# x tiles on multiples of 512 bytes, and another order of small work around them: a gated linear-attention layer on one Trainium2 core

## The chip, the cores and the metric

The kernel runs on one core of one Trainium2 chip. The metric is the device time of one execution in microseconds. The engines are TensorE (PE; its weight loads are listed apart as PEld), VectorE (DVE), ScalarE (ACT), GpSimd (POOL) and SyncE (SP), which issues most of the DMAs. L1160 means line 1160 of the kernel before.

## The reference

The input x has 2,048 tokens of 640 features. It is normalised per token, and two branches read the result:

```python
xn = _layernorm(x, axis=-1)
s = _A_ref(xn, A_wqkv, A_w_phi, A_wo)
g = _silu(_B_ref(xn, B_w1, B_b1, B_w2, B_b2))
return x + s * g
# _A_ref: 32 heads of 20
pq = jnp.einsum("bhsd,hdf->bhsf", q, w_phi)      # the same for k
phi_q = jnp.concatenate([_softmax(pq, axis=-1), _softmax(-pq, axis=-1)], axis=-1)
kv = jnp.einsum("bhsf,bhsd->bhfd", phi_k, v)
z  = jnp.einsum("bhsf->bhf", phi_k)
o = phi_q kv / (phi_q z + 1e-6)                  # then @ wo
# _B_ref: 640 -> 1536 -> 640
h = _gelu(jnp.einsum("bsd,df->bsf", x, w1) + b1)
return jnp.einsum("bsf,fd->bsd", h, w2) + b2
```

All inputs and outputs are fp32.

## The kernel before, in words

Every fp32 operand of a large product is split into a high and a low part, and each product is done in three passes (high by high, high by low, low by high: `PASSES`). Many products are done by a block scheme that needs sums of blocks of x and of the weights and fewer matmuls: a `Unit` with the steps s1 to s7 in the first stage and the query stage, seven `PARTS` in the feed-forward units.

The transposed, normalised x and its block sums lie in two tiles that stay on the chip for most of the run: `xp` (8 blocks, high and low, 512 columns each) and `xd` (9 blocks, in the place of the folded weights `folds`). A small unused tile, `xpad`, stands ahead of them in their pool. A partition of the on-chip memory is filled in this order: constants, 23 slabs of 5,120 bytes, 11 rows of 2,816 bytes, the small tiles, then `xpad`, `xp`, `xd`. By the tiles' sizes xp begins at byte 158,656 of a partition, which is 309 x 512 + 448. Late in the run the x pool is closed, and an equal pad, `lpad`, and the pool `late` (13 tiles of up to 5,120 bytes) take the place: the output weights `wo` and every second set of `oT` lie there.

The stages, in time:

- The first stage (to about 180 us) folds w_phi into the weights, normalises and transposes x, and makes keys, values and the state `kv`. `turn` transposes and splits a pair of tokens' tiles, `t_sums`, `t_hi` and `t_lo` make the block sums in xd, `weight_sums` (`vw`, `kw`) and `weight_forms` (`kform`, `vform`) those of the weights. `norm_a`, `norm_b` and `norm_apply` are the statistics and the application of the layer norm.
- The query stage (to about 249 us) makes the query features: a maximum (`q_max`, `p_max`), a negation (`f_neg`), a subtraction (`q_sub`, `p_sub`), an exponential and a store (`q_put`). Four tiles are done plainly (`query_plain`), the others in units.
- The gated stage (to about 577 us) runs 12 feed-forward units. Each has 54 matmuls in `part` (L1160: x streams past the weights `w1s`) and 60 in `down` (L1189: `hs` streams past `w2s`).
- The output stage runs four chunks of 512 tokens. `finish` (L1361) streams `oT` past `wo`; `oT` of the first and third chunk lies in `late`, that of the second and fourth in slabs.

The order of work is written out by hand: under the manual schedule every engine and queue does its work in the order of the program. A unit calls `slot(i)` between its steps, and tables (`k_side`, `v_side`, `q_side`, `first_q`, `second_q`, `mid_q`) say which small work goes into which slot. SyncE's loads and stores are a queue of that kind too. In a unit, cx1 (L499), cu2 (L502) and c22 (L505, L506) read the bank of a step before a later step writes it.

Of the kernel before, what the change touches and what calls it, by code (L numbers as in the profile page):

```python
# [45 lines left out]
def hedgehog_gated_mlp_kernel(ctx: ExitStack, tc: tile.TileContext, x, xt_in, wqk, bd, wv, wo, w1, b1, w2, b2, out_t):  # L46
# [6 lines left out]

    xstack = ExitStack()
    xpool = xstack.enter_context(tc.tile_pool(name="xpool", bufs=1))
    xpool.tile([P, 16], F32, name="xpad")
    xp = xpool.tile([P, 8, 2, CW], F32R, name="xp")
    foldt = xpool.tile([P, 2 * KC * 6 * P + 6 * 120], F32, tag="D", name="folds")
    folds = foldt[:, :2 * KC * 6 * P].rearrange("p (w c i t) -> p w c i t", w=2, c=KC, i=6)
# [24 lines left out]
    def bankA():  # L84
        return pools["A"].tile([P, 2, 512], F32, tag="A", name="pA")
# [177 lines left out]
    def t_hi(q):  # L263
        nc.scalar.activation(xd()[:, :, 0, at(q)], tts[q][:], AF.Copy)

    def t_lo(q):
        tt, dst = tts.pop(q), xd()[:, :, :, at(q)]
        nc.gpsimd.tensor_tensor(dst[:, :, 1, :], tt[:], dst[:, :, 0, :].bitcast(F32), op=OP.subtract)

    def turn(q, part, ps=None):  # L270
        if part == 0:
            xrs[q] = slab(F32, "xr", (P, KC, W2))[:]
        xr = xrs[q]
        if ps is None:
            ps = bankW()[:]
        srcs = [(0, k) for k in range(4)] if part == 0 else [(1, k) for k in range(4)] if part == 1 else [(0, 4), (1, 4)]
        for i, (o, k) in enumerate(srcs):
            nc.tensor.transpose(ps[:, i * P:(i + 1) * P], xns[2 * q + o][:, k * P:(k + 1) * P], ident[:])
        v = ps.rearrange("p (k t) -> p k t", t=P)
        if part == 0:  # L280
            raw, src, dst = xr[:, 0:4, :P], v, xp[:, 0:4, :, at(q)]
        elif part == 1:
            raw, src, dst = xr[:, 0:4, P:], v, xp[:, 5:7, :, at(q)]
        else:
            raw, src, dst = xr[:, 4, :].rearrange("p (k t) -> p k t", t=P), v[:, :2], xp[:, 4::3, :, at(q)]
            xns.pop(2 * q), xns.pop(2 * q + 1)
        hi = src[:, 2:4] if part == 1 else src
        nc.scalar.activation(dst[:, :, 0, :], hi, AF.Copy)
        nc.scalar.activation(raw, src, AF.Copy)
        nc.vector.tensor_tensor(dst[:, :, 1, :], hi, dst[:, :, 0, :].bitcast(F32), op=OP.subtract)  # L290
# [97 lines left out]
    def key_fin(ef, at=None):  # L388
        ss = head_sums(ef, "rc")
        rc = ss[:] if at is None else at  # L390
        nc.vector.reciprocal(rc, ss[:])
        scale_heads(ef, rc, nc.gpsimd if at is None else nc.vector)
        return ef
# [339 lines left out]
    vw = weight_sums(rv01, rv23)  # L733
    fold_q(3)
    phis[2] = key_fin(es.pop(2), tiny[:, 64:128])
    turn(2, 2, bankA()[:, 0])
    x_in(8)
    x_in(9)
    t_sums(2)
    next(vw)  # L740
    norm_a(7)
    kv_acc(1, phis.pop(1), vs.pop(1))
    fold_q(4)
    es[3] = feat1(pk, tiny[:, 32:64])
    t_hi(2)
    t_lo(2)
    next(vw)
    vs[3] = value(3)
    next(kform)
    feat2(es[3])  # L750
    norm_b(7)
    next(vw)
# [52 lines left out]
    def k_acc(p):  # L805
        for o in range(2):
            kv_acc(2 * p + o, flat(uk[p].out[o]), uv[p].out[o])
        del uk[p], uv[p]
# [15 lines left out]
    def k_side(p):  # L824
        o = p - 1
        if p == 2:
            return {
                0: [(x_in, 10), (k_form,)],
                1: [(turn, 3, 0), (turn, 3, 1), (v_form,), (v_rows, 2)],
                3: [(turn, 3, 2), (k_form,), (x_in, 11)],  # L830
                5: [(t_sums, 3), (norm_a, 8), (v_form,)],
            }
        if p == 3:
            return {
                0: [(k_neg, 2, 0), (k_max, 2, 0, True), (x_in, 13), (turn, 4, 2), (k_neg, 2, 1), (t_sums, 4)],
                1: [(v_rows, 3)],
                2: [(k_sub, 2, 0, nc.vector), (k_max, 2, 1, False), (x_in, 12), (t_hi, 4), (norm_apply, 11), (t_lo, 4), (k_sub, 2, 1, nc.gpsimd)],
                4: [(norm_apply, 10), (k_exp, 2, 0)],
                5: [(k_sum, 2, 0)],
                6: [(k_scale, 2, 0)],  # L840
            }
        return {
            0: [(k_acc, p - 2), (k_neg, o, 0), (k_neg, o, 1), (k_max, o, 0, True), (p < 7 and t_sums, p + 1), (p == 7 and load_rq,)],
            1: [(p == 4 and x_in, 14), (p == 4 and x_in, 15)],
            2: [(k_sub, o, 0, nc.vector), (v_rows, p), (k_max, o, 1, False), (p < 7 and t_hi, p + 1), (k_sub, o, 1, nc.gpsimd)],
            4: [(p < 7 and t_lo, p + 1), (k_exp, o, 0)],
            5: [(k_sum, o, 0), (k_scale, o, 0)],
        }

    def v_side(p):  # L850
        o = p - 1
        if p == 2:
            return {
                0: [(norm_b, 8)],
                1: [(acc3,), (norm_a, 9), (t_hi, 3), (norm_apply, 8)],
                3: [(norm_b, 9), (t_lo, 3)],
                4: [(spill, 2), (norm_apply, 9), (norm_a, 10), (v_form,)],
                5: [(norm_a, 11), (turn, 4, 0)],
                6: [(norm_b, 10), (turn, 4, 1), (v_form,), (norm_b, 11)],
            }  # L860
        if p == 3:
            return {
                0: [(turn, 5, 0), (norm_a, 12)],
                1: [(k_exp, 2, 1)],
                2: [(k_sum, 2, 1), (k_scale, 2, 1), (turn, 5, 1)],
                3: [(norm_b, 12), (norm_a, 13)],
                4: [(norm_b, 13), (turn, 5, 2)],
                5: [(norm_apply, 12), (norm_apply, 13), (spill, 3)],
            }
        return {  # L870
            0: [(p < 6 and turn, p + 2, 0), (p == 4 and norm_a, 14), (k_exp, o, 1)],
            2: [(k_sum, o, 1), (p < 6 and turn, p + 2, 1)],
            3: [(k_scale, o, 1), (p == 4 and norm_b, 14), (p == 4 and norm_a, 15)],
            5: [(p == 4 and norm_apply, 14), (p < 6 and turn, p + 2, 2), (p == 4 and norm_b, 15)],
            6: [(p == 4 and norm_apply, 15)],
        }
# [37 lines left out]
    def q_side(q):  # L914
        e0, e1 = uq[q].out
        return {
            0: [(f_neg, e0), (f_neg, e1), (q_max, e0, (q, 0)), (q_sub, e0, (q, 0), nc.gpsimd)],
            2: [(q_max2, q)],
            3: [(q_sub, e1, (q, 1), nc.vector)],
            4: [(q_put, e0, 2 * q)],  # L920
            5: [(q_put, e1, 2 * q + 1)],
        }

# [34 lines left out]
    def wq_form(n):  # L958
        t = slab(F32R, "wsum")
        t4 = t[:].rearrange("p b (k c) -> p b k c", k=2)  # L960
        for k in range(2):
            src = {"S1": rq[k][:, HALF:], "S2": sums["st"][:, 1, k * HALF:(k + 1) * HALF],
                   "S3": sums["st"][:, 0, k * HALF:(k + 1) * HALF], "S4": rq[2 + k][:, :HALF]}[n]
            split_sum(src, [t4[:, b, k] for b in range(2)], nc.gpsimd)
        sums[n] = [lambda b, t4=t4, i=i: t4[:, b, i] for i in range(2)]
# [12 lines left out]
    def p_max(t, psum=False):  # L978
        f_neg(pl[t])
        q_max(pl[t], t, pls[t][:, HALF:HALF + 64] if psum else None)  # L980
# [36 lines left out]
    k_exp(o, 1)  # L1017
    k_sum(o, 1)
    wq_form("S2")
    pl[2] = query_plain(2)  # L1020
    q_put(pl[0], 0)
    k_scale(o, 1)
    p_max(1, True)
    p_sub(1, nc.vector)
    pl[3] = query_plain(3)
    q_put(pl[1], 1)
    wq_form("S1")
    p_max(2, True)
    p_sub(2, nc.vector)
    wq_form("S4")  # L1030
    k_acc(o)
    w1r = load_w1(0)
    fq = {}
# [12 lines left out]

    def first_q():
        return {
            0: [(p_max, 3, True)],
            1: [(q_put, pl[2], 2), (p_sub, 3, nc.vector)],  # L1050
            5: [(q_put, pl[3], 3)],
            6: [(w1_step,)],
        }

    def second_q():
        return {
            2: [(w1_step,)],
            5: [(kv_end,)],
        }

    def mid_q(i):
        q = order[i - 2]
        e0, e1 = uq[q].out
        return {
            0: [(f_neg, e0), (f_neg, e1), (q_max, e0, (q, 0)), (q_sub, e0, (q, 0), nc.gpsimd)],
            2: [(q_max2, q), (w1_step,)],
            3: [(q_sub, e1, (q, 1), nc.vector)],
            4: [(q_put, e0, 2 * q)],
            5: [(q_put, e1, 2 * q + 1), (i == 2 and load_xq, 3)],
        }  # L1070

    fq.update(wq_forms())
# [17 lines left out]
    slot(2)  # L1090
    u.s3()
    u.cu2()
    slot(3)
    slot(4)
    w.s6()
    w.c21()
    u.s4()
    slot(5)
    u.s5()
    u.c22()  # L1100
    f_neg(ea[0])
    q_max(ea[0], 0)
    q_sub(ea[0], 0, nc.gpsimd)
# [301 lines left out]
    for unit in range(units):  # L1405
# [79 lines left out]
        if not more:  # L1485
            phin = load_phi(ORDER[1])
            xstack.close()
            ctx.enter_context(tc.tile_pool(name="pad", bufs=1)).tile([P, 16], F32, name="lpad")
            late = ctx.enter_context(tc.tile_pool(name="late", bufs=13, reuse_waits="tile"))
        w1f = w1_forms(w1r) if more and not back else none  # L1490
        if back:
# [125 lines left out]
```

## Time and profile before

| | |
|---|---|
| time, median of 3 runs | 682.1 us (680.92 to 682.28) |
| the profiled execution's own time | 681.68 us |
| its span, first to last instruction | 679.9 us |
| granted TensorE clock over the span | 0.997 |
| PE, DVE, ACT, POOL busy | 98%, 67%, 47%, 58% |
| DMA | 129.60 MB, 191 GB/s over the span |

The span is what the trace shows; the time of the execution has 1.8 us more around it. A timeline or chain row gives a start and a length in us, the engine, the line, the tile written and the tiles read, and the number of instructions that were merged; a bracket behind it gives the idle time of the engine ahead of it and what ended that. A row of the chain of waits gives the total, the number and the longest in us.

### The profile page before, as it was taken

To read this page: it belongs to the slowest core of one execution; us is meant where nothing else is said; L and a number is where in the kernel's file an instruction comes from. 1 tells how busy PE (TensorE), PEld (TensorE's weight loads), DVE (VectorE), ACT (ScalarE), POOL (GpSimd) and SP (SyncE) were. 2 spreads that over 40 slices of the span, in tenths; PEclk is the share of its full clock that TensorE was granted. 3 is DMA by queue.
4 is the path that set the end of the run, shared out by engine and by line. 5 is a ranking of instruction groups with operands and counts; after the bars stand their busy time and mean duration, and the time that the engine had idled before them with its cause. 6 is when DMAs were issued, how large, how long until landed. Compare 5 with 4: busy or idle time off the path is not lost.

```text
span 679.9 us, 11969 instructions
## 1 busy us (share of the span) xinstructions
PE 667.8 (98%) x4615; PEld 576.5 (85%) x4615; DVE 453.3 (67%) x716; ACT 322.8 (47%) x552; POOL 391.9 (58%) x341
## 2 busy tenths in 40 slices
PE   9999899999999999999999999999999999999997
PEld 9999799999999987888888888888888886777875
DVE  4968897766775657485875775767867876333232
ACT  3556676654566667534244147632132346645220
POOL 2777787765774442956875844636357665322232
PEclk9999899999999999999999999999999999999999
DMA  8436560032732881719657595296375185657444
GB/s 332 174 117 195 171 182 10 2 98 80 210 117 98 286 325 49 266 60 320 220 174 278 209 425 240 65 366 227 133 278 196 76 323 200 227 182 274 151 149 139
DMA packets 76408, 129.60 MB, mean 191 GB/s; under 512 B 4768, under 2 KB 44192, under 8 KB 75456
## 3 DMA queue, kind: packets, MB, share of 16 engines
q1 hardware_dynamic: 76032, 128.19, 53.4%
q10 hardware_dynamic: 320, 0.66, 0.5%
q8 instruction: 36, 0.59, 0.4%
q14 instruction: 20, 0.16, 0.1%
HBM read 81.97 MB, written 46.20 MB: 189 GB/s over the span
## 4 chain that ended last, share of the span: by engine, by line
PE 90%; POOL 3%; ACT 2%; DVE 2%; issue 2%; DMA 1%; DVEq 0%; ACTq 0%; POOLq 0%
PE pB L1189 24%; PE pB L1160 22%; PE pW L453 18%; PE pB L1361 10%; PE pA L312 3%; PE pB L1292 3%; PE pW L936 2%; PE pB L1281 2%; PE pA L157 2%; PE kv L547 1%; DMA xq<-xp_dram 1%; PE pA L623 1%; POOL rk L655 1%; POOL tt L249 1%; POOL wv L132 1%
## 5 line engine op out<-in xcount | busy, mean ns | idle before, releaser
L1189 PE MATMUL pB<-hs,w2s 128*128 128x512 f32 x720 | 167.8, 391 | 0.0
L1189 PEld LDWEIGHTS pB<-hs,w2s 128*128 128x128 f32 x720 | 134.5, 188 | 30.2 <-issue 1.2
L1160 PE MATMUL pB<-xp,w1s 128*128 128x512 f32 x324 | 83.3, 394 | 0.0
L1160 PE MATMUL pB<-xd,w1s 128*128 128x512 f32 x324 | 81.4, 394 | 0.0
L1160 PEld LDWEIGHTS pB<-xd,w1s 128*128 128x128 f32 x324 | 60.6, 187 | 15.0
L1160 PEld LDWEIGHTS pB<-xp,w1s 128*128 128x128 f32 x324 | 60.6, 187 | 14.7
L1198 DVE TENSOR_TENSOR y<-pB,y 128x512 f32<-128x512 f32 x100 | 63.8, 680 | 12.8 <-PE pB L1189 12.7
L1361 PE MATMUL pB<-oT,wo 128*128 128x512 f32 x300 | 72.1, 395 | 0.0
L370 POOL TENSOR_TENSOR eq<-eq,rc 128x1280 f32<-128x1280 f32 x16 | 37.9, 2370 | 58.8 <-DVE rc L1260 51.2
L1165 ACT ACTIVATE pB<-pB,b1t 128x512 f32<-128x512 f32 x48 | 31.8, 662 | 78.7 <-DVE pB L1461 26.9
L1361 PEld LDWEIGHTS pB<-oT,wo 128*128 128x128 f32 x300 | 55.4, 188 | 15.0 <-DVE oT L1296 1.2
L351 POOL TENSOR_TENSOR e<-e,mxs 128x1280 f32<-128x1280 f32 x13 | 30.7, 2369 | 56.3 <-ACT e L357 18.5
L453 PE MATMUL pW<-wsum,xd 128*128 128x320 f32 x288 | 49.4, 310 | 1.2 <-DVE wsum L419 1.0
L571 POOL TENSOR_TENSOR w1s<-raw,w1s 128x640 fp32r<-128x640 f32 (+1 forms) x18 | 24.4, 1356 | 42.2 <-ACT w1s L570 42.2
L1247 POOL TENSOR_TENSOR ez<-eq,zrep 128x1280 f32<-128x1280 f32 x16 | 47.3, 2955 | 0.0
L357 ACT ACTIVATE e<-e 128x1280 f32<-128x1280 f32 x32 | 40.7, 1271 | 13.0 <-DVE e L351 4.6
L453 PEld LDWEIGHTS pW<-wsum,xd 128*128 128x128 f32 x288 | 43.6, 188 | 1.8 <-DVE wsum L419 1.2
L1176 ACT ACTIVATE x<-pB 128x512 f32<-128x512 f32 x12 | 7.2, 598 | 75.4 <-PE pB L1160 75.4
L1284 ACT ACTIVATE ph<-pB 120x512 f32<-120x512 f32 (+1 forms) x48 | 23.6, 561 | 34.8 <-PE pB L1281 31.7
L370 POOL TENSOR_TENSOR e<-e,rc 128x1280 f32<-128x1280 f32 x15 | 36.1, 2406 | 6.3 <-DVE rc L799 3.0
L1171 DVE TENSOR_TENSOR hs<-pB,hs 128x512 fp32r<-128x512 f32 x48 | 32.0, 685 | 5.4 <-ACT hs L1167 5.4
L1367 POOL TENSOR_TENSOR xres<-y,xres 128x256 f32<-128x256 f32 x20 | 14.2, 732 | 35.8 <-DVE y L1366 17.4
(204 smaller groups left out, 1322.0 us busy)
## 6 DMA issues: line engine op xcount, KB each, us to landing
raw<-in_w_dram SPq DMA_DIRECT2D x42, 320.0 KB, 5.5
e_dram<-e SPq DMA_DIRECT2D x16, 640.0 KB, 3.5
eq<-e_dram SPq DMA_DIRECT2D x16, 640.0 KB, 7.5
phi_dram<-eq SPq DMA_DIRECT2D x16, 640.0 KB, 3.3
phi<-phi_dram SPq DMA_DIRECT2D x16, 640.0 KB, 8.0
xt<-in_x_dram SPq DMA_DIRECT2D x16, 320.0 KB, 5.8
xres<-in_xt_dram SPq DMA_DIRECT2D x20, 256.0 KB, 5.4
out_dram<-xres SPq DMA_DIRECT2D x18, 256.0 KB, 4.8
```

The costliest lines, as they stand in the source:

```text
L351: eng.tensor_tensor(e3, e3, mx[:, :, None].to_broadcast([P, 64, DH]), op=OP.subtract)
L357: nc.scalar.activation(ef, ef, AF.Exp)
L370: eng.tensor_tensor(e3, e3, rc[:, :, None].to_broadcast([P, 64, DH]), op=OP.mult)
L453: nc.tensor.matmul(self.bank[ch][:, :HALF], self.x(blk, a), w(b), start=new and i == 0, stop=i == len(mms) - 1, skip_group_check=True)
L571: nc.gpsimd.tensor_tensor(sl[:, 1, :n], src, sl[:, 0, :n].bitcast(F32), op=OP.subtract)
L1160: nc.tensor.matmul(bank[ch][:], tl[:, a, off + wo_:off + wo_ + P], mov(blk, b), start=new and n == 0, stop=n == len(mms) - 1, skip_group_c ...
L1165: nc.scalar.activation(ps, ps, AF.Gelu_apprx_tanh, bias=b1t[:, f:f + 1])
L1171: nc.vector.tensor_tensor(hs[:, 1], ps, hs[:, 0].bitcast(F32), op=OP.subtract)
L1189: nc.tensor.matmul(ps[:], ws[i][:, b, d * P:(d + 1) * P], hs[o][i][:, a, :], start=i == n == 0, stop=(i, n) == (GF - 1, 2), skip_group_che ...
L1198: nc.vector.tensor_tensor(y, ps[:], y, op=OP.add)
L1247: nc.gpsimd.tensor_tensor(zv, ef, zf, op=OP.mult)
L1361: nc.tensor.matmul(ps[:], w, o, start=n == 0, stop=n == 14)
```

## The change

The pads ahead of the x tiles and of `late` grow from 16 to 32 floats, so that xp, xd and the tiles of `late` begin at multiples of 512 bytes of a partition. The rest puts existing work in another order:

- first stage: two steps of the value weights' sums (`next(vw)`) and one of the key weights' forms (`next(kform)`) earlier; `norm_apply(11)` ahead of `t_hi(4)`; `acc3` one slot earlier; `turn(4, 0)` ahead of `norm_a(11)`;
- query stage: `p_max(1)` ahead of `query_plain(2)`, the form S1 behind S4, `p_sub(3)` and `kv_end` one slot earlier, one negation of a unit in slot 1, `load_xq(3)` ahead of a `q_put`, and in the last unit `u.s5` ahead of `u.s4` and c22 ahead of slot 5.

```diff
-    xpool.tile([P, 16], F32, name="xpad")
+    xpool.tile([P, 32], F32, name="xpad")
...
     phis[2] = key_fin(es.pop(2), tiny[:, 64:128])
+    next(vw)
     turn(2, 2, bankA()[:, 0])
     x_in(8)
     x_in(9)
     t_sums(2)
-    next(vw)
     norm_a(7)
...
     t_hi(2)
+    next(vw)
     t_lo(2)
-    next(vw)
+    next(kform)
     vs[3] = value(3)
-    next(kform)
...
-                2: [(k_sub, 2, 0, nc.vector), (k_max, 2, 1, False), (x_in, 12), (t_hi, 4), (norm_apply, 11), (t_lo, 4), (k_sub, 2, 1, nc.gpsimd)],
+                2: [(k_sub, 2, 0, nc.vector), (k_max, 2, 1, False), (x_in, 12), (norm_apply, 11), (t_hi, 4), (t_lo, 4), (k_sub, 2, 1, nc.gpsimd)],
...
-                0: [(norm_b, 8)],
-                1: [(acc3,), (norm_a, 9), (t_hi, 3), (norm_apply, 8)],
+                0: [(acc3,), (norm_b, 8)],
+                1: [(norm_a, 9), (t_hi, 3), (norm_apply, 8)],
...
-                5: [(norm_a, 11), (turn, 4, 0)],
+                5: [(turn, 4, 0), (norm_a, 11)],
...
-            3: [(q_sub, e1, (q, 1), nc.vector)],
-            4: [(q_put, e0, 2 * q)],
+            4: [(q_sub, e1, (q, 1), nc.vector), (q_put, e0, 2 * q)],
...
     wq_form("S2")
+    p_max(1, True)
     pl[2] = query_plain(2)
     q_put(pl[0], 0)
     k_scale(o, 1)
-    p_max(1, True)
     p_sub(1, nc.vector)
     pl[3] = query_plain(3)
     q_put(pl[1], 1)
-    wq_form("S1")
     p_max(2, True)
     p_sub(2, nc.vector)
     wq_form("S4")
+    wq_form("S1")
     k_acc(o)
...
-            0: [(p_max, 3, True)],
-            1: [(q_put, pl[2], 2), (p_sub, 3, nc.vector)],
+            0: [(p_max, 3, True), (p_sub, 3, nc.vector)],
+            1: [(q_put, pl[2], 2)],
...
-            5: [(kv_end,)],
+            4: [(kv_end,)],
...
-            0: [(f_neg, e0), (f_neg, e1), (q_max, e0, (q, 0)), (q_sub, e0, (q, 0), nc.gpsimd)],
+            0: [(f_neg, e0), (q_max, e0, (q, 0)), (q_sub, e0, (q, 0), nc.gpsimd)],
+            1: [(f_neg, e1)],
...
-            5: [(q_put, e1, 2 * q + 1), (i == 2 and load_xq, 3)],
+            5: [(i == 2 and load_xq, 3), (q_put, e1, 2 * q + 1)],
...
     u.s3()
     u.cu2()
-    slot(3)
     slot(4)
     w.s6()
     w.c21()
+    u.s5()
+    slot(3)
     u.s4()
+    u.c22()
     slot(5)
-    u.s5()
-    u.c22()
...
-            ctx.enter_context(tc.tile_pool(name="pad", bufs=1)).tile([P, 16], F32, name="lpad")
+            ctx.enter_context(tc.tile_pool(name="pad", bufs=1)).tile([P, 32], F32, name="lpad")
```

## The prediction

> **What bounds the kernel now.** I read the page first: the busy table, then the chain that ended last.
>
> ```profile
> PE 667.8 (98%) x4615; PEld 576.5 (85%) x4615; DVE 453.3 (67%) x716; ACT 322.8 (47%) x552; POOL 391.9 (58%) x341
> PE 90%; POOL 3%; ACT 2%; DVE 2%; issue 2%; DMA 1%; DVEq 0%; ACTq 0%; POOLq 0%
> PE pB L1189 24%; PE pB L1160 22%; PE pW L453 18%; PE pB L1361 10%; PE pA L312 3%; PE pB L1292 3%; PE pW L936 2%; PE pB L1281 2%; PE pA L157 2%; PE kv L547 1%; DMA xq<-xp_dram 1%; PE pA L623 1%; POOL rk L655 1%; POOL tt L249 1%; POOL wv L132 1%
> ```
>
> TensorE is busy for 667.8 of 679.9 us, so time can come from two places only: from the spacing of its matmuls, or from its few waits. The number of matmuls does not change. So I looked first at the spacing, in the chain in order of time and in the timeline of PE.
>
> ```profile
> 141.33 16.04 PE pW L453 x108
> 179.07 13.57 PE pW L936 x90
> 369.20 13.62 PE pB L1189 x60
> 382.82 12.60 PE pB L1160 x54
> 395.73 12.64 PE L1189 MATMUL pB<-hs,w2s 128*128 128x512 f32 x55
> 655.77 2.20 PE L1361 MATMUL pB<-oT,wo 128*128 128x512 f32 x9
> 659.66 15.50 PE L1361 MATMUL pB<-oT,wo 128*128 128x512 f32 x67
> ```
>
> Rows 3 and 4 have the same shape, 128x512 moving and 128x128 stationary. L1189 takes 13.62/60 = 227.0 ns each, L1160 12.60/54 = 233.3 ns. A timeline row ends with the last matmul's own 0.39 us, so its spacing is (12.64 - 0.39)/54 = 226.9 ns for L1189, (2.20 - 0.39)/8 = 226 ns for the first L1361 row (the third chunk of the output stage) and (15.50 - 0.39)/66 = 228.9 ns for the second (the fourth chunk).
>
> Where the operands start explains all four. The tile sizes in the code (small pool 2,688 bytes, rows 11 x 2,816, slabs 23 x 5,120 from a multiple of 512) put xp, xd and every tile of `late` 448 bytes past a multiple of 512, and every slab on a multiple. L1189 streams a slab past slab weights (0 against 0). L1361's third chunk streams a `late` tile past `late` weights (448 against 448). Both run at 226 to 227. L1361's fourth chunk streams a slab past `late` weights (0 against 448): 228.9. L1160 streams x past slab weights (448 against 0): 233.3. Equal offsets are fast, unequal ones are slow, in either direction but not by the same amount. With 320 columns I see no such cost: L453, with x as the stationary operand at 448, takes 16.04/108 = 148.5 ns with its changes of line, L936 with slabs for both 150.8.
>
> The waits come next (PE's rows of the chain of waits):
>
> ```profile
> PE pW L453 <- DVE e L506: 2.3, 2, 2.2
> PE pA L623 <- POOL ones L106: 1.2, 1, 1.2
> PE pW L453 <- DVE wsum L419: 1.0, 1, 1.0
> PE pW L453 <- ACT u L499: 0.9, 2, 0.7
> PE pW L453 <- DMA xq<-xp_dram: 0.9, 1, 0.9
> ```
>
> L506's 2.2 and L419 lie in the first stage, L499's two and the DMA in the query stage. Without L623, the first matmul of all, they are 5 us, and no order of small work can gain much more.
>
> **Part 1, the padding: 64 to 128 bytes.** It adds no instruction. xp moves from byte 158,656 of a partition to 158,720 = 310 x 512, xd (32,768 behind it) likewise, and all of `late`, whose pad stands at the same place.
>
> L1160: 648 matmuls (324 on xp, 324 on xd, 54 in each of 12 units) go from 233.3 to L1189's 226.9. That is 54 x 6.4 = 0.35 us a unit, 12 x 0.35 = **-4.2 us**. They stand on the path for 12.60 us a unit and PE's chain of waits has nothing in the units, so all of it counts if the other engines follow; by the busy table each of them is idle for a third of the span or more. The bounds are 0 (offset is not the cause) and 648 x 7.3 = -4.7 (226 ns, the fastest row). I take the row of the nearest kind, both at 0.
>
> L1361: chunks 2 and 4 (150 matmuls) go from 0 against 448 to 0 against 0: 150 x 2.0 = **-0.3 us**. Chunks 1 and 3 keep equal offsets: 0.
>
> The 320-column matmuls: rows of both kinds give no difference, so 0; the bounds are the spread of the two rows, 2.3 ns on about 1,050 with x as weights, ±2.4 us. I take 0, because the row with slabs is the slower one only through its 2 us of weight changes between banks.
>
> [...]
>
> **Part 2, the query stage.** These rows are from the timeline, by engine.
>
> ```profile
> 193.82 0.55 DVE L799 RECIPROCAL rc<-rc 128x64 f32<-128x64 f32 x1
> 194.93 1.50 DVE L346 TENSOR_REDUCE pW<-e 128x64 f32<-128x1280 f32 x1 [0.56 <-ACT e L342]
> 198.04 1.27 ACT L357 ACTIVATE e<-e 128x1280 f32<-128x1280 f32 x1 [0.53 <-DVE e L351]
> 201.92 0.41 ACT L499 ACTIVATE u<-pW 128x320 f32<-128x320 f32 x1
> 202.38 1.15 PE L453 MATMUL pW<-wsum,xd 128*128 128x320 f32 x6 [0.22 <-ACT u L499]
> 203.63 1.49 DVE L346 TENSOR_REDUCE pW<-e 128x64 f32<-128x1280 f32 x1
> 205.42 1.48 DVE L351 TENSOR_TENSOR e<-e,pW 128x1280 f32<-128x1280 f32 x1
> 207.00 1.28 ACT L357 ACTIVATE e<-e 128x1280 f32<-128x1280 f32 x1 [1.59 <-DVE e L351]
> 208.65 1.15 PE L453 MATMUL pW<-wsum,xq 128*128 128x320 f32 x6 [0.72 <-ACT u L499]
> 219.41 1.84 SPq L912 DMA_DIRECT2D e_dram<-e  x2
> 221.35 0.41 SPq L896 DMA_DIRECT2D xq<-xp_dram  x1
> 223.11 1.72 SPq L896 DMA_DIRECT2D xq<-xp_dram  x1
> 229.50 1.29 PE L453 MATMUL pW<-wq,xq 128*128 128x320 f32 x7 [0.90 <-DMA xq<-xp_dram]
> 246.02 0.60 PE L453 MATMUL pW<-wq,xq 128*128 128x320 f32 x3
> 246.66 1.58 PE L453 MATMUL pW<-wq,xd 128*128 128x320 f32 x9
> ```
>
> `p_max(1)` ahead of `query_plain(2)`: its ScalarE negation leaves the place after the exponential at 193 and fills an idle stretch near 191. VectorE's maximum then starts right behind the reciprocal, at 194.4 rather than 194.93, and the chain maximum, subtraction, exponential, weight copies, L499 follows: -0.5 us at 201.92. PE's wait at 202.38 (0.22 idle, 0.37 beyond the 147 ns spacing) goes. In this chain S1 behind S4 moves the negation of tile 2 forward by two copies (0.81 us); S1's split still ends near 203, its first user is PE at 205.6.
>
> `p_sub(3)` in slot 0: the subtraction no longer stands behind c11 (0.48 us on VectorE); with tile 2's earlier negation it ends near 205.4 instead of 206.90. The exponential at 207.00 follows, and L499 behind it on ScalarE: about 207.0 instead of 208.18. PE wants it at 207.4, so the 0.72 idle (0.88 with spacing) goes. c11 comes 0.3 us later; PE does not wait for its bank here.
>
> `load_xq(3)` ahead of `q_put(e1)`: on SyncE four loads stood behind the second store of 219.41, which waited for an exponential. They go out 1.5 us sooner; the store waits behind four issues of 0.4 to 1.7 us, and nobody reads its rows before the gated stage. The third load ended PE's 0.90 (1.06 with spacing) at 229.50; 1.5 covers it. Two of the four slabs are freed by PE at 219.1, in time. Late next is nothing that the trace shows.
>
> `u.s5` ahead of `u.s4`, and c22 ahead of the second exponential, let VectorE free bank C sooner: the matmul at 246.66 could start at 246.02 + 3 x 0.147 = 246.46, -0.15 with a rest kept. The empty slot 3, `kv_end` (slot 5 to 4: it passes matmuls and c21 on VectorE, while its own fills and copies are on GpSimd and ScalarE, so no queue changes its order) and the split negation in `mid_q` (0.73 us of ScalarE behind L499, while c11 waits for the maximum anyway) cost nothing.
>
> Sum: 0.37 + 0.88 + 1.0 + 0.15 = **-2.4 us**; bounds 0 and -3 (all query waits gone).
>
> **Part 3, the first stage.**
>
> ```profile
> 51.19 1.44 POOL L249 TENSOR_TENSOR tt<-xr 128x256 f32<-128x256 f32 x2 [4.48 <-ACT xr L289]
> 57.71 1.56 POOL L404 TENSOR_TENSOR ws<-rv 128x640 f32<-128x640 f32 x1
> 60.27 2.70 POOL L268 TENSOR_TENSOR xd<-tt,xd 128x1152 fp32r<-128x1152 f32 x1 [0.50 <-ACT xd L264]
> 61.00 2.02 DVE L335 TENSOR_TENSOR tiny<-mn,mx 128x32 f32<-128x32 f32 x1
> 68.20 2.96 POOL L370 TENSOR_TENSOR e<-e,rc 128x1280 f32<-128x1280 f32 x1
> 76.16 1.16 ACT L264 ACTIVATE xd<-tt 128x1152 fp32r<-128x1152 f32 x1 [4.05 <-POOL tt L249]
> 75.87 0.99 PE L453 MATMUL pW<-wsum,xd 128*128 128x320 f32 x5 [0.96 <-DVE wsum L419]
> 79.03 2.77 PE L453 MATMUL pW<-wk,xd 128*128 128x320 f32 x9 [2.17 <-DVE e L506]
> 82.78 0.88 DVE L180 BATCH_NORM_STATS2 st<-xt 128x6 f32<-128x320 f32 x2
> 90.00 1.29 PE L453 MATMUL pW<-wv,xd 128*128 128x320 f32 x7 [0.22 <-DVE v L506]
> ```
>
> PE's 2.17 ends with c22, which stood behind `t_hi(3)` on ScalarE (76.16), which stood behind GpSimd's sums. GpSimd is nearly gapless from 57.3 to 76.6. The first `next(vw)` (1.56) now fills the 4.48 before 51.19, the second goes ahead of `t_lo(2)`. GpSimd comes out 0.8 us ahead, but `t_lo(2)` itself ends 0.7 later, and L335 (2.02; 0.58 without the company) ended with it; the keys' exponential and reciprocal, for which L370 waits, follow. Of 0.8 I keep 0.2. `kform` ahead of `value(3)` saves VectorE an idle 0.35, within that delay. `acc3` ahead of `s2` makes PE wait up to 1 us for L370's result at 71.1, but PE waits until 79.03 anyway: 0. `turn(4, 0)` ahead of `norm_a(11)` leaves VectorE idle until ScalarE's copies at 83.65 instead of doing 1.3 us of statistics; it is gapless afterwards to the L506 of 89.94, so PE's 0.22 at 90.00 grows by about 0.4. `norm_apply(11)` fills ScalarE's wait before `t_hi(4)`: 0. Sum **+0.2 us**; bounds -1.5 (the whole `next(vw)` reaches 79.03) and +0.8 (both delays in full).
>
> **Sum.** -4.2 - 0.3 - 2.4 + 0.2 = -6.7. The profiled execution took 681.68 us (span 679.9 and 1.8 around it), 0.4 below the median of 682.1: 681.68 - 6.7 = **675.0 us**.
>
> **Rivals.**
> *The offset does not matter*: x lies in another part of the memory than the slabs, and L1361's slow chunk too streams between the two parts; so region and offset can't be told apart by these rows alone. Against it: the two mixed cases differ (228.9, 233.3), which two regions alone need not give. Then 675.0 + 4.5 = 679.5. [...]
> *The query waits come back*: ScalarE is bound by the exponentials, and PE meets the next one as late. Speaks for it: margins of 0.3 to 0.5 us. Against it: each moved step has an idle stretch to go to. 675.0 + 2.4 = 677.4.
> *Slower*: two streams that start at the same place of 512 bytes collide, and 64 bytes of distance kept L1160 out of it; it rises above 233.3. With parts 2 and 3 at -2.2 it is slower by over 0.2% (683.5) from 648 matmuls x 6.2 ns, 239.5 ns on; at 241 it gives 684.5. Against it stand L1189's slabs, equal at 0, at 226.9.
>
> **How the numbers follow.** Forecast 0.70, its own range 673.0 to 677.0 (first stage -1.5, fastest row; and +0.8 with a query wait left). Offset without effect 0.16, query waits back 0.09, slower 0.05. About 0.2%, 1.4 us, is what a measurement of this kernel can tell from no change. Faster: 0.70, 0.09 of the second (679.5 is 0.4% below the median, its spread reaches across the bound) and 0.08 of the third, 0.87; same 0.07; slower 0.06. The range 673.0 to 679.8 takes in the first three.
>
> **What would show it.** L1160 x54 at 12.25 us instead of 12.60, L1361's last chunk near 227 ns; L499 and the xq load gone from PE's waits; L506's wait near 2.0 and L419's near 1 to 1.5. Wrong: L1160 at 12.6 or above, or new waits of PE for L499's line between 200 and 250 us.

## The result, and the profile after

The changed kernel takes 672.86 us (median of 4 executions, 672.09 to 673.72), the kernel before on the same chip 682.01 us (median of 4, 680.92 to 682.28): a ratio of 0.9869 (95% interval 0.9851 to 0.9887), or 9.15 us less. The profiled execution took 673.72 us with a span of 672.0 us, 7.96 and 7.9 us less than those of before. It is the slowest of the four; the last point of the comparison with the prediction is on why the medians lie further apart.

The page after, the busy table and the chain that ended last by engine:

```profile
PE 662.2 (99%) x4615; PEld 577.1 (86%) x4615; DVE 452.6 (67%) x716; ACT 322.8 (48%) x552; POOL 391.8 (58%) x341
PE 93%; POOL 4%; DVE 1%; issue 1%; ACT 0%; POOLq 0%; DVEq 0%
```

PE's instructions are as many as before, its busy time is 5.6 us less, and its share of the chain is 93% instead of 90%. The chain in order of time (start, length in us, then engine, line and count) shows where most of the 5.6 us come from:

```profile
141.03 16.04 PE pW L453 x108
377.70 12.24 PE pB L1160 x54
389.94 13.60 PE pB L1189 x60
441.99 14.03 PE pB L1189 x60
646.62 20.64 PE pB L1361 x90
```

L1160's 54 matmuls take 12.24 us, 226.7 ns each; they took 12.60. The 108 matmuls of 320 columns still take 16.04, so they gained nothing. The fourth row is one feed-forward unit, the eighth, in which L1189 takes 0.43 us more than in the others; in that unit it took 13.78 before. The last row is the end of the output stage, 20.64 us.

PE's rows of the chain of waits:

```profile
PE pW L453 <- DVE e L506: 2.3, 2, 2.2
PE kv L547 <- POOL e L370: 0.3, 1, 0.3
PE pW L453 <- DVE v L506: 0.2, 1, 0.2
```

The waits for L499, for the xq load and for L419 are gone from this list. L506's 2.2 is still there. The wait of L547 for L370 is new.

By stage, from the starts of the same matmuls in the two profiled executions:

| stretch (start after) | gain or loss, us | predicted |
|---|---|---|
| start, to 42.8 us | +0.37 | 0 |
| first stage, to 89.7 | -0.64 | +0.2 |
| rest of the first stage, and the query stage, to 246.3 | -3.0 | -2.4 (all of it in the query stage) |
| feed-forward units, to 569.9 | -4.25 | -4.2 |
| output stage, to the end | -0.4 | -0.3 |
| sum | -7.9 | -6.7 |

### The profile page after: what moved, and what is told of

It reads as the page before. It is cut to its first block, busy times and chain, and to the rows that moved or that the text cites. A ratio compares the mean times of both kernels' runs of the same rounds, so it can differ in the third digit from the quotient of the medians.

```text
span 672.0 us, 11968 instructions
## 1 busy us (share of the span) xinstructions
PE 662.2 (99%) x4615; PEld 577.1 (86%) x4615; DVE 452.6 (67%) x716; ACT 322.8 (48%) x552; POOL 391.8 (58%) x341
## 4 chain that ended last, share of the span: by engine, by line
PE 93%; POOL 4%; DVE 1%; issue 1%; ACT 0%; POOLq 0%; DVEq 0%
PE pB L1189 25%; PE pB L1160 22%; PE pW L453 19%; PE pB L1361 10%; PE pA L312 3%; PE pB L1292 3%; PE pW L935 3%; PE pB L1281 2%; PE kv L547 1%; PE pA L157 1%; PE pA L623 1%; POOL rk L655 1%; POOL tt L249 1%; PE pW L278 1%; POOL wv L132 1%
## 5 line engine op out<-in xcount | busy, mean ns | idle before, releaser
L1189 PE MATMUL pB<-hs,w2s 128*128 128x512 f32 x720 | 167.8, 391 | 0.0
L1189 PEld LDWEIGHTS pB<-hs,w2s 128*128 128x128 f32 x720 | 134.5, 188 | 30.2 <-issue 1.2
L1160 PE MATMUL pB<-xp,w1s 128*128 128x512 f32 x324 | 81.2, 389 | 0.0
L1160 PE MATMUL pB<-xd,w1s 128*128 128x512 f32 x324 | 79.3, 389 | 0.0
L1160 PEld LDWEIGHTS pB<-xd,w1s 128*128 128x128 f32 x324 | 60.8, 188 | 12.6
L1361 PE MATMUL pB<-oT,wo 128*128 128x512 f32 x300 | 71.6, 394 | 0.0
L1160 PEld LDWEIGHTS pB<-xp,w1s 128*128 128x128 f32 x324 | 60.8, 188 | 12.6
L370 POOL TENSOR_TENSOR eq<-eq,rc 128x1280 f32<-128x1280 f32 x16 | 37.9, 2369 | 57.6 <-DVE rc L1260 50.3
L1361 PEld LDWEIGHTS pB<-oT,wo 128*128 128x128 f32 x300 | 55.4, 188 | 14.5 <-ACT oTl L1300 1.2
L453 PE MATMUL pW<-wsum,xd 128*128 128x320 f32 x288 | 49.0, 311 | 0.0
L453 PEld LDWEIGHTS pW<-wsum,xd 128*128 128x128 f32 x288 | 43.6, 188 | 0.2 <-DVE wsum L419 0.2
L370 POOL TENSOR_TENSOR e<-e,rc 128x1280 f32<-128x1280 f32 x15 | 36.1, 2408 | 5.6 <-DVE rc L799 2.6
```

The source lines that it names most:

```text
L370: eng.tensor_tensor(e3, e3, rc[:, :, None].to_broadcast([P, 64, DH]), op=OP.mult)
L453: nc.tensor.matmul(self.bank[ch][:, :HALF], self.x(blk, a), w(b), start=new and i == 0, stop=i == len(mms) - 1, skip_group_check=True)
L1160: nc.tensor.matmul(bank[ch][:], tl[:, a, off + wo_:off + wo_ + P], mov(blk, b), start=new and n == 0, stop=n == len(mms) - 1, skip_group_c ...
L1189: nc.tensor.matmul(ps[:], ws[i][:, b, d * P:(d + 1) * P], hs[o][i][:, a, :], start=i == n == 0, stop=(i, n) == (GF - 1, 2), skip_group_che ...
L1361: nc.tensor.matmul(ps[:], w, o, start=n == 0, stop=n == 14)
```

## The experiments

**Which part gives what.** First the two parts of the change apart: the kernel before with both pads alone, and the changed kernel with both pads set back.

```diff
# pads_only, against the kernel before
-    xpool.tile([P, 16], F32, name="xpad")
+    xpool.tile([P, 32], F32, name="xpad")
...
-            ctx.enter_context(tc.tile_pool(name="pad", bufs=1)).tile([P, 16], F32, name="lpad")
+            ctx.enter_context(tc.tile_pool(name="pad", bufs=1)).tile([P, 32], F32, name="lpad")
```

> The kernel before with the two pads at 32 floats and nothing reordered. Theory (start offsets modulo 512 set the matmul spacing): L1160 at 12.24 us for 54 in each unit, L1361's last chunk near 227 ns, the waits of PE at L499, the xq load and 75.87 us as in the kernel before; 4.6 us less than before, about 677.4. Rival (the order of the small work lets the units run faster, the pads do nothing): L1160 stays at 12.60, within 0.5 us of before.

Measured: 677.55 us (677.23 to 678.23, 5 executions) against 682.06, ratio 0.9929 (0.9915 to 0.9943), 4.5 us less. L1160 takes 12.24 us for 54 in every unit. PE's waits of this kernel:

```profile
PE pW L453 <- DVE e L506: 2.3, 2, 2.2
PE pW L453 <- DMA xq<-xp_dram: 1.3, 1, 1.3
PE pW L453 <- DVE wsum L419: 1.0, 1, 1.0
PE pW L453 <- ACT u L499: 0.9, 2, 0.7
```

They are the waits of the kernel before, so the pads take none away, and the 4.5 us are spacing. The wait for xq is 0.4 us longer here, and the eighth unit's L1189 takes 14.21 instead of 13.78: so a part of what the spacing gains is lost there.

```diff
# order_only, against the changed kernel
-    xpool.tile([P, 32], F32, name="xpad")
+    xpool.tile([P, 16], F32, name="xpad")
...
-            ctx.enter_context(tc.tile_pool(name="pad", bufs=1)).tile([P, 32], F32, name="lpad")
+            ctx.enter_context(tc.tile_pool(name="pad", bufs=1)).tile([P, 16], F32, name="lpad")
```

> The changed kernel with both pads back at 16 floats. Theory: L1160 at 12.60 us for 54, L1361 as before, but PE's waits for L499, for the xq load and for L419 at 75.9 us gone; 3 us less than before in the query stage and 0.3 to 0.6 in the first stage, about 678.5. Rival (the pads do everything, the removed waits come back elsewhere): within 0.5 us of before.

Measured: 677.68 us (676.95 to 678.87, 6 executions), ratio 0.9932 (0.9919 to 0.9946), 4.4 us less. Its chain of work and its waits:

```profile
378.27 12.60 PE pB L1160 x54
649.64 20.83 PE pB L1361 x90
```

```profile
PE pW L453 <- DVE e L506: 2.3, 2, 2.2
PE pW L453 <- DVE v L506: 0.5, 1, 0.5
PE kv L547 <- POOL e L370: 0.3, 1, 0.3
```

L1160 and L1361 are as before the change, and the waits for L499, the load and L419 are gone. The time is 0.8 us below the 678.5 that was expected. 4.5 + 4.4 = 8.9, the whole 9.15 within what the two can tell: the parts add up, and neither needs the other. No run takes the moves of the second part one by one; how they share the 4.4 us is read from the trace alone.

**Is it the difference between the operands?** The prediction read the spacing as a matter of where the moving operand starts against the weights. The output stage tests that without x: with only `lpad` set back, the tiles of `late` lie 448 bytes past a multiple of 512 and the slabs on one, so its last chunk streams at 0 past weights at 448, as before.

```diff
# x_pad_only, against the changed kernel
-            ctx.enter_context(tc.tile_pool(name="pad", bufs=1)).tile([P, 32], F32, name="lpad")
+            ctx.enter_context(tc.tile_pool(name="pad", bufs=1)).tile([P, 16], F32, name="lpad")
```

> The changed kernel with the pad ahead of the late pool back at 16 floats: x at a multiple of 512, the output weights and the first and third oT 448 past one. Theory (equal offsets are fast): L1160 stays at 12.24, the fourth output chunk goes back from 227 to 229 ns a matmul (20.83 us for the last 90 instead of 20.64), 0.3 to 0.4 us more than the changed kernel. Rival (the output stage gained by something else): its rows stay as in the changed kernel.

Measured: 673.91 us (673.48 to 674.47, 4 executions), ratio 0.9877 (0.9863 to 0.9891). Its chain:

```profile
377.55 12.24 PE pB L1160 x54
646.66 20.83 PE pB L1361 x90
```

L1160 is fast, the last 90 of L1361 are back at 20.83: each follows its own pad. The profiled execution is 0.25 us longer than that of the changed kernel, near the expected 0.3 to 0.4; the medians differ by 1.05, which the pad does not explain.

Then x at other places, with the weights of L1160 left on a multiple of 512, and one kernel in which everything stands 448 past. The last is made in the tile ahead of all pools.

```diff
# x_64: 48, x_128: 64, x_192: 80, x_256: 96
-    xpool.tile([P, 32], F32, name="xpad")
+    xpool.tile([P, 48], F32, name="xpad")
# all_448
-    const.tile([P, 24], F32, name="align")
+    const.tile([P, 8], F32, name="align")
```

> The changed kernel with a pad of 48 floats instead of 32 in front of x: x starts 64 bytes past a multiple of 512, the slabs with the weights of L1160 on a multiple, the late tiles as in the changed kernel. First reading: the difference of the starts, moving operand minus weights, modulo 512 bytes sets the spacing. It is 64 here, as it was in the kernel before's last chunk of L1361 (0 against 448), so L1160 takes 229 ns, 12.35 to 12.38 us for 54, and the kernel about 674.3 us (648 x 2.3 ns = 1.5 over 672.9). Second reading: what counts is whether the moving operand itself lies on a multiple of 512; then 64 is as bad as 448: 233.3 ns, 12.60 us for 54, about 677.1 us. Third: the cost goes with the distance to the nearest multiple of 512; 64 and 448 are equally far, so 12.60 too. A price between 12.38 and 12.60 would fit none of the three.

> The changed kernel with a pad of 64 floats in front of x: x starts 128 bytes past a multiple of 512, the weights of L1160 on a multiple. If the price repeats every 256 bytes and grows with the difference (64: 229.2 ns, 192: 233.3), 128 lies between: 229 to 233 ns, 12.38 to 12.60 us for 54, 674.3 to 677.1 us. If only odd multiples of 64 cost, or only the two neighbours of the weights' place, 128 is free: 12.24 us, 672.9 us.

> The changed kernel with a pad of 80 floats in front of x: x starts 192 bytes past a multiple of 512, the weights of L1160 on a multiple. So far L1160 took 226.7 ns at a difference of 0 and of 256 bytes, 229.2 at 64 and 233.3 at 448. If the price repeats every 256 bytes, 192 equals 448 (448 - 256 = 192): 12.60 us for 54 and about 677.1 us. If it is a price of starting within 64 bytes of the weights' place modulo 512 on either side, 192 is far from both 0 and 512 and free: 12.24 us, 672.9 us.

> The changed kernel with a pad of 96 floats in front of x: x starts 256 bytes past a multiple of 512, the weights of L1160 on a multiple. If the period is 512 bytes, L1160 stays dearer than 226.7 ns: between 229 and 240 ns, 12.4 to 12.95 us for 54, since half the period is the largest distance; the kernel between 674.5 and 681. If the period is 256 or 128 bytes (448 is off both), 256 is as good as 0: 12.24 us for 54 and 672.9 us. If what matters is only a 64 byte step against the weights, as for 448, the price is 12.60 again.

> The changed kernel with 64 bytes taken from the alignment tile in front of all pools, so that x, the slabs and the late tiles all start 448 bytes past a multiple of 512: all equal among themselves, none on a multiple. If the difference between the two operands decides, nothing changes: L1160 x54 12.24, L1189 x60 13.60, last 90 of L1361 20.64, the kernel 672.9 us within 0.8. If a start on a multiple of 512 is what each operand needs, L1160 goes to 12.60 (+4.3 us) and L1189's 720 matmuls rise as well (by 2 to 6.6 ns, +1.4 to +4.7 us), L1361's 300 likewise (+0.6 to +2): 679 to 684 us.

Measured, one profiled execution each: 675.28, 676.33, 676.65, 674.39 and 674.42 us. The rows of one unit in the chain of each, in the same order:

```profile
378.02 12.38 PE pB L1160 x54
390.40 13.65 PE pB L1189 x60
```

```profile
378.15 12.59 PE pB L1160 x54
```

```profile
378.37 12.60 PE pB L1160 x54
```

```profile
378.21 12.24 PE pB L1160 x54
```

```profile
378.24 12.24 PE pB L1160 x54
390.48 13.60 PE pB L1189 x60
647.32 20.64 PE pB L1361 x90
```

Divided by 54, with the rows of before and after the change in between:

| moving start minus weights' start, modulo 512 bytes | modulo 256 | ns a matmul |
|---|---|---|
| 0 (changed kernel; all_448; L1189) | 0 | 226.7 |
| 64 (x_64; L1361's last chunk before, 0 against 448) | 64 | 229.3; 228.9 |
| 128 (x_128) | 128 | 233.1 |
| 192 (x_192) | 192 | 233.3 |
| 256 (x_256) | 0 | 226.7 |
| 448 (kernel before) | 192 | 233.3 |

Three things follow. The kernel all_448 settles that a multiple of 512 has no worth in itself: with nothing on one, all three lines stay at their fast times. x_64 settles that the sign of the difference counts: at the same distance from a multiple of 512 as before the change, x costs 229.3 and not 233.3, the price that L1361 paid at a difference of 64. The reading by the distance alone, and that by the moving operand's place alone, fall; both expected 12.60. And the price repeats every 256 bytes in all that was tried: 256 is as good as 0, 192 as dear as 448. Of the two readings for x_192 the other, a price for the neighbours of the weights' place alone, falls. Differences of 320 and 384, and steps under 64 bytes, were not tried; what makes the period is not shown.

The totals of these single executions say less than the spacing. x_128 lies within its range and x_192 0.45 below its 677.1. x_256 and all_448 lie 1.5 above 672.9, but 0.7 above the changed kernel's profiled execution; matched matmul by matmul, both lose 0.6 to 0.7 us at the load of xq, where PE waits 0.4 and the profiled execution of the changed kernel does not. x_64 lies 1.0 above its 674.3, and 1.56 above that execution: it is 2.1 slower in the units (L1160's 0.14 in each, and L1189 at 13.65 instead of 13.60 us in eight of them), loses 0.4 at the load of xq, and is 0.9 faster for a stretch of slow clock which it does not have (1.00 granted from 79 to 84 us, against 0.68; the last point of the comparison with the prediction). So all_448 missed its expected 672.9 within 0.8, on waits and not on spacing.

**The wait that stayed.** PE's 2.17 us in front of 78.67 ends with c22 of a unit, which in slot 0 and 1 stands behind statistics on VectorE and behind `t_hi(3)` on ScalarE. I put these steps behind c22:

```diff
# c22_free, against the changed kernel
-                0: [(acc3,), (norm_b, 8)],
-                1: [(norm_a, 9), (t_hi, 3), (norm_apply, 8)],
+                0: [(acc3,)],
+                2: [(norm_b, 8), (norm_a, 9), (t_hi, 3), (norm_apply, 8)],
```

> The changed kernel with norm_b(8), norm_a(9), t_hi(3) and norm_apply(8) moved from slots 0 and 1 to slot 2 of the second value unit, behind c11 and c22. Theory (PE's 2.17 us at 78.7 us is c22 queued on ScalarE behind t_hi(3), which waits for GpSimd's sums, and on VectorE behind norm_b(8)): PE's wait for L506 falls from 2.2 to below 0.3 us, no half-clock window near 79 us, 2 to 3.5 us less than the changed kernel, near 670. Rival (the wait only moves: the transposes of tile 8 wait for norm_apply(8), which still ends near 77.8): PE waits 1 to 1.5 us at L278 instead, gain below 1 us, clock window kept.

Measured: 673.57 us (672.95 to 674.27, 4 executions), ratio 0.9872 (0.9857 to 0.9886), no better than the changed kernel's 0.9869. PE's waits:

```profile
PE pW L453 <- ACT e L512: 1.3, 1, 1.3
PE pW L453 <- DVE v L506: 1.0, 1, 1.0
PE pA L157 <- DMA folds<-in_wqk_dram: 1.0, 1, 1.0
PE pB L1189 <- ACT hs L1167: 0.8, 1, 0.8
PE pW L453 <- DVE e L506: 0.2, 1, 0.2
```

The 2.17 is gone, as the theory had it. 1.26 of it comes back at 81.49, where ScalarE's L512 is late behind the work that was moved, and 0.8 more than in the changed kernel at 88.34. That is what the rival said in kind, a wait that moves, though not at L278, and the slow clock that the rival kept is gone (1.00 granted from 79 to 84 us, where the changed kernel's profile has 0.68). PE is 1.4 us ahead there (88.34 against 89.73), but 0.9 of it is the slow clock of the changed kernel's profile, so the edit itself left 0.4 of the 2.17. At 246 the lead is 1.1. At 443.73 it loses 0.96 of that, to L1189's wait for ScalarE's `hs` in the unit that took 14.03 before (15.0 here, and not the 14.4 that is said below): it comes to the stage earlier and waits there longer. (The 1.0 for the folds costs nothing against the changed kernel: the matmuls ahead of it ended sooner, and the one behind it starts at 7.48 against 7.54.) The chain of this kernel names what `hs` waited for:

```profile
434.02 8.98 DMA g_dram<-y
443.08 0.61 ACT hs L1167
443.73 12.13 PE pB L1189 x51
```

ScalarE waits for a transfer: the five stores of the gate's tiles end at 443.0, and the next `hs` takes the slab of one of them. They are issued at 434.02 though the tiles were complete near 423. SyncE's queue holds them up, as its own rows of the chain of waits of the changed kernel (from 400 to 446 us) show:

```profile
SPq L1232 <- POOL bdk L1117: 26.1, 1, 26.1
```

It stands for 26.1 us at the store of phi, L1232, which waits for GpSimd; the five stores are behind it in the program. So I moved them ahead of it, in the changed kernel (g_early) and together with the edit above (both):

```diff
# g_early, against the changed kernel
-        if unit == NG + 1:
-            for d, o in enumerate(held):
-                nc.sync.dma_start(g_dram[d], o[:])
...
         silu(3)
+        if unit == NG:
+            for d, o in enumerate(held):
+                nc.sync.dma_start(g_dram[d], o[:])
```

> The changed kernel with two more edits. acc3 alone in slot 0 and the three statistics steps of slots 0 and 1 in slot 2 of the same table, which took the 2.17 us wait at 78.67 away but was given back elsewhere; and the five stores of g_dram ahead of the store of phi in the unit before, since SyncE's queue stands for 26.1 us at that store (for GpSimd's bdk) and the five stores behind it keep the slabs that the gelu of the next unit needs: L1189 took 14.03 us there instead of 13.60 (and 14.4 with the first edit). Theory (the stores are the cause): L1189 x60 takes 13.60 in every unit from the second on, the wait for hs is gone, and the kernel is 0.4 to 0.8 us faster than with the first edit alone: 672.9 (672.2 to 673.3), 9.2 us less than before. Rival: the wait is ScalarE's, which is late with the gelu of that unit in any case; then L1189 stays at 14.0 or more and the time at 673.6. A second rival is that the five stores, issued earlier, meet the loads of that unit and make something else late: 674 or more.

> The changed kernel with one edit, the five stores of g_dram issued ahead of the store of phi for which SyncE's queue stands for 26.1 us. If these stores alone made L1189 take 14.03 us in that unit, it takes 13.60 there now and the kernel 672.4 (0.43 less than 672.9), with the 2.17 us wait at 78.67 and, in a part of the executions, the slow clock behind it left as they were. If the stores only matter together with the first edit, L1189 stays at 14.0 and the time at 672.9. Of the 672.1 of the two edits together, the first edit would then account for 0.3 or for 0.8.

Measured: both 672.09 us (671.82 to 672.41, 4 executions) against 682.03, ratio 0.9856 (0.9840 to 0.9873); g_early 672.27 us (672.06 to 672.50, 4 executions) against 682.33, ratio 0.9852 (0.9835 to 0.9868). g_early is near its expected 672.4, both is 0.1 below its range. In the chain of g_early, and then of both, the unit in question:

```profile
441.18 13.60 PE pB L1189 x60
```

```profile
440.51 13.60 PE pB L1189 x60
```

The theory of the stores holds: 13.60 in both, and the wait for `hs` is gone. It also holds without the first edit, so 0.43 us of the changed kernel's profiled execution was this queue. The rivals, ScalarE late in any case and loads disturbed, fall. Medians below the kernel before are 10.06 (g_early) and 9.94 us (both) against 9.15, but the intervals of the ratios overlap with the changed kernel's: the profile shows the 0.43, the times alone don't. g_early and both differ by the edit of c22: in the profiles both is 0.67 us ahead from 90 us on, 0.24 of it from the start of the kernel and 0.43 from the edit; the medians, 672.27 and 672.09, can't tell that.

## Why the prediction was right, and where not

The direction, the likeliest case and both halves were right; the size was too small. The median of 672.86 lies 0.1 below the 673.0 at which the range of the likeliest case began, the profiled 673.72 inside. By the prediction's own steps:

**L1160, -4.2: right.** 12 x (12.60 - 12.24) = 4.32 us of spacing, and pads_only has 4.5 in all. The feed-forward units gave 4.25: L1189 gained another 0.02 in most of them, and the eighth gave 0.25 back (14.03 against 13.78). The mechanism, equal starts of the two operands, holds as well, with a period of 256 bytes where the prediction took 512. The prediction saw no wait of PE in the units and took it that the other engines follow; in one unit a queue of stores did not, and the page's shares of busy time could not show that.

**L1361, -0.3: right.** The last chunk's 90 take 20.64 instead of 20.83 us, x_pad_only shows that it is this pad, and the stage gave 0.4.

**The 320-column matmuls, 0: right.** 16.04 us for 108 before and after. The reason given, 2 us of weight changes in the row of L936, is not in its trace: all but a few of L936's matmuls follow each other at 146 to 147 ns and L453's at 145 to 149, and three near 181 us are late by 0.3 us together, where a weight load waits 0.23 us for VectorE's `wq` (L132).

**The rival of the offset without effect** fell with x_64 and all_448. In x_64 x lies in the same part of the memory as in the changed kernel, 64 bytes on, and L1160 takes 229.3 ns instead of 226.7; in all_448 x starts 448 bytes past a multiple of 512 as in the kernel before, but so do the weights, and L1160 takes 226.7 ns instead of 233.3. At 128x512 the place of one operand against the other changes the spacing by up to 6.6 ns in these runs, 233.3 against 226.7; why it does, no run shows. *The slower case*, a collision at equal places, fell too: equal places are the fast ones, 226.7 ns on a multiple of 512 (the changed kernel) and off it (all_448).

**The query stage, -2.4: right in each step, a little small.** PE's stretches after:

```profile
201.70 1.04 PE L453 MATMUL pW<-wsum,xd 128*128 128x320 f32 x6
206.98 1.04 PE L453 MATMUL pW<-wsum,xq 128*128 128x320 f32 x6
226.34 2.36 PE L453 MATMUL pW<-wq,xq 128*128 128x320 f32 x15
243.49 1.48 PE L453 MATMUL pW<-wq,xd 128*128 128x320 f32 x9
```

These are the rows of the four places that the prediction named (202.38, 208.65, 229.50, 246.66 before), and none has a bracket: PE no longer waits at them. The lead over the kernel before grows there by 0.41, 1.12, 1.06 and 0.20 us, 2.8 together against 2.4, with some 0.2 in steps too small to place. The rival that the waits come back fell here: L506 at 238.55 with 0.17 is the only wait left in this stage. But the third place is tighter than this trace shows. Of the ten other traces in which PE has the same matmuls in the same order, nine lose 0.13 to 0.67 us against this one at the matmuls behind the load of xq, so 0.4 to 1.1 us of this wait was saved, and not 1.0 in each.

**The first stage, +0.2: this step failed.** The changed kernel gained 0.64 there. PE's timeline:

```profile
70.83 0.84 PE L547 MATMUL kv<-e,v 128*32 128x40 f32 x64 [0.33 <-POOL e L370]
73.03 1.92 PE L453 MATMUL pW<-wsum,xd 128*128 128x320 f32 x12
75.23 1.27 PE L453 MATMUL pW<-wsum,xd 128*128 128x320 f32 x6
78.67 2.64 PE L453 MATMUL pW<-wk,xd 128*128 128x320 f32 x9 [2.17 <-DVE e L506]
89.73 1.43 PE L453 MATMUL pW<-wv,xd 128*128 128x320 f32 x8 [0.22 <-DVE v L506]
```

GpSimd, ScalarE and VectorE in the same stretch:

```profile
61.38 0.19 DVE L335 TENSOR_TENSOR tiny<-mn,mx 128x32 f32<-128x32 f32 x1
67.83 2.95 POOL L370 TENSOR_TENSOR e<-e,rc 128x1280 f32<-128x1280 f32 x1
75.80 1.17 ACT L264 ACTIVATE xd<-tt 128x1152 fp32r<-128x1152 f32 x1 [3.98 <-POOL tt L249]
74.50 0.95 DVE L419 TENSOR_TENSOR wsum<-ws,wsum 128x640 fp32r<-128x640 f32 x1
78.13 0.49 DVE L506 TENSOR_TENSOR e<-u,pW 128x320 f32<-128x320 f32 x1
```

The failed step is "of 0.8 I keep 0.2", GpSimd's lead. The prediction gave the rest up for L335, which took 2.02 before and was to end late with `t_lo(2)`, and for the keys' reciprocal behind it. But L335 takes 0.19 here, the reciprocal is done at 67.22, ahead of GpSimd's own sums (67.87), and GpSimd goes from these to L370 without a wait. It starts L370 at 67.83 instead of 68.20, and the kernel's start is 0.37 us later, so it is 0.74 ahead. ScalarE's `t_hi(3)` (75.80 instead of 76.16) and VectorE's L506 (78.13 instead of 78.48) follow it, and PE goes on at 78.67 instead of 79.03, 0.73 ahead of the same start and not 0.2. What PE loses on the way it would have waited for L506 anyway: `acc3`, moved ahead, costs it 0.33 at 70.83, and L419, which ends at 75.45, some 0.2 in the third row (1.27 us, where six such matmuls take 1.04), and the wait for L506 is still 2.17. L419's wait, which the prediction let stand at 1 to 1.5, is all but gone.

The second failure is the price of `turn(4, 0)` ahead of `norm_a(11)`, +0.4 at 90.00: the last row still has 0.22, and from 78.67 to it PE needs 0.1 more than before (11.06 against 10.97). 0.5 of the one and 0.3 of the other are the 0.84 us between +0.2 and -0.64. The second holds for these two profiles, both with a slow clock in this stretch (0.67 and 0.68 granted from 79 to 84 us); in the five traces of the same order without it this wait is 0.49 to 0.52, and no trace of the kernel before shows what it would be there.

**The start: +0.37, not foreseen**, in work that the change does not touch: the first matmul that needs the load of the folds starts at 7.54 instead of 7.26 us. In the thirteen traces of this study it starts between 6.91 and 7.81, with the same matmuls ahead of it, so a difference of some tenths at the start says nothing about the change.

**From the profiled 673.72 to the median 672.86.** Behind the 2.17 us wait, the granted clock of the changed kernel's profile falls (PEclk, the third number from the end of the row, as a share of the full clock):

```profile
74.00:79.00 5.00, 2.83 (x18) 2.34 (x17) 3.81 (x13) 2.62 (x4) 3.02 (x5) 0.98 0.42 130
79.00:84.00 5.00, 5.00 (x27) 4.95 (x27) 3.71 (x9) 2.96 (x5) 3.49 (x2) 0.68 0.00 0
```

The second of these windows in order_only, with the same wait of 2.2:

```profile
79.00:84.00 5.00, 4.87 (x36) 4.61 (x36) 4.47 (x12) 4.59 (x10) 3.04 (x3) 1.00 0.00 0
```

At 0.68 PE does 27 matmuls in these 5 us, at 1.00 it does 36. What that is worth is seen beside the rows at 78.67 and 89.73 above; in the chain of order_only they are:

```profile
78.13 1.58 PE pW L453 x9
88.30 3.79 PE pW L453 x24
```

The first nine matmuls take 2.64 instead of 1.58 us, and from the first row to the second it is 11.06 against 10.17 us: the slow stretch costs 0.9 us here, which is not made up later in the stage. The same distance is 10.14 to 10.17 in the five traces at full clock and 11.06 to 11.19 in the four of this order at the low one. Of the eleven kernels that keep this wait (the kernel before among them) six show the low clock in their profile (0.66 to 0.74 in the second window) and five do not (1.00); c22_free and both, which have no such wait, have 1.00. The kernel before's profile has it too (0.67), so the two profiled executions compare like with like: -6.7 predicted, -7.9 measured. The medians lie 9.15 apart, since the profile of before is 0.33 below its median and that of after 0.86 above. Of the changed kernel's four executions, two have a mean granted clock of 1.0 and spans of 670.4 and 670.6, two have 0.995 and 0.997 and spans of 672.0 and 671.6. That the stretch makes 0.9 of this difference fits, but is not shown for executions without a trace: in g_early the execution at 0.995 has a span only 0.5 longer than the one at 1.0. In finer windows of the changed kernel's profile the granted clock is 0.50 from 78.85 to 82.2 us and 1.00 just ahead of it (78.75 to 78.80) and behind it (82.25 to 82.30): a stretch of about 3.4 us, which begins some 0.2 us after the wait has ended at 78.67. In the profile of the kernel before it is 0.50 between the same two times, and begins some 0.2 us ahead of the end of the wait, at 79.03. What sets the length, and why the stretch is there in six traces and not in five with the same wait, no run shows.

## What to carry to other kernels

Where one line of matmuls has a larger spacing than another of the same shape (here 233.3 against 227.0 ns at 128x512), compare where the moving operand and the weights start in a partition: in these runs a difference of 0 modulo 256 bytes gave 226.7 ns and the others 228.9 to 233.3, and 16 floats more in the pad in front of a pool were enough to make it 0. That was found at 512 columns; at 320 columns, with x as the weights, it made no difference (16.03 to 16.04 us for 108 at every place tried). When a moved step removes a wait, see what waits close behind it (in c22_free 0.4 of 2.17 us were left, since ScalarE's L512 then ended a new wait of 1.26); and after a gain look once more at the queues, since a store held up behind another store's wait can take a part of the gain back hundreds of microseconds later (here 0.43 us near 443 us, from a queue that stood for 26.1 us).

## What the runs showed of the hardware that I had not expected

At 128x512, with new 128x128 weights for each matmul, the price of a difference in start repeats every 256 bytes in all that was tried and is not symmetric: 0, 2.6, 6.4 and 6.6 ns a matmul at 0, 64, 128 and 192. The difference of a multiple of 512 that the change aims at is more than is needed. At 320 columns, with x as the weights, 108 matmuls take 16.03 to 16.04 us at each of these places. And around the end of a wait of 2.17 us the granted clock fell in six of eleven traces, to a mean of 0.66 to 0.74 from 79 to 84 us; in the changed kernel's profile it was 0.50 for about 3.4 us, and that cost 0.9 us.
